# An attention and feed-forward kernel: the one-element tile of its first exponential moves into a longer identity tile, and every large buffer starts at another address

## The chip, the cores and the metric

The kernel runs on one core of a Trainium2 chip. The time is the device time of one execution in microseconds (us); a measurement is the median of several runs. TensorE, VectorE, ScalarE, GpSimd and SyncE are written PE, DVE, ACT, POOL and SP, as in the profile. The on-chip buffer (SBUF) has 128 partitions. A tile has the same address in all of them, and all addresses below are bytes from the start of a partition.

## The reference

Eight batches, eight heads, 576 tokens, head dimension 64, all in fp32. First 32 packed queries attend over the keys, then the tokens attend over the 32 packed results, and a feed-forward layer with a SiLU follows:

```
def sm_attn(qq, kk, vv):
    s = scale * np.matmul(qq, kk.transpose(0, 1, 3, 2))
    s = s - np.max(s, axis=-1, keepdims=True)
    a = np.exp(s)
    a = a / (np.sum(a, axis=-1, keepdims=True) + 1e-09)
    return np.matmul(a, vv)
p_packed = sm_attn(p, k, v)
out = sm_attn(q, p_packed, p_packed)
...
h = x @ w_in                      # x: 4608 x 512, w_in: 512 x 2048
g = h * (1.0 / (1.0 + np.exp(-h)))
return (g @ w_out)                # w_out: 2048 x 512
```

Here `x` is `out` with the heads side by side, so that the two large products of the feed-forward layer do most of the arithmetic. The weights `w_in` and `w_out` come in as 64-bit floats.

## The kernel before, in words

**Tiling.** A batch's 576 tokens are two halves of 288. The feed-forward dimension of 2048 is 16 slices of 128. The kernel multiplies the packed results of a batch with `w_in` once (`Packs.products`, L221) and gets the tiles `pw_hi` and `pw_lo`: fp32 values split in two parts, so that one product is made of three matmuls (high with high, high with low, low with high). A unit of work is one batch and one slice of 128:

- `h_products` (L501) makes the hidden values of the 2 x 288 tokens in PSUM. The stationary operand is a 128x128 block of `pw_hi` or `pw_lo`; the moving one is a row of 288 columns of `a2_hi` or `a2_lo`, the attention's shares. For a half these are six matmuls, three for `par` 0 and three for `par` 1, and `par` picks the first or the second 288 columns of the `a2` tile.
- `h_values` and `h_lower` (L519 to L526) apply the SiLU on ACT and split the result into `g_hi` and `g_lo`, on ACT and DVE.
- `out_products` (L533) adds the slice to the output sums in `ps_acc`. The stationary operand is a 128x128 block of `g_hi` or `g_lo`; the moving one is a row of 512 columns of `wo_hi` or `wo_lo`.

**Stages.** The first part, up to about 140 us, loads the weights in chunks (`Weights.fetch`, L183), turns the 64-bit floats into fp32 on ACT and DVE (L189 to L202) and splits `w_out` into `wo_hi` and `wo_lo` (L210, L214). Beside this run the attention of the first batches and the units of the first eight blocks. From then on the feed-forward units of a batch run with steps of the next batch's attention between them. The attention of every batch but the first spreads its turned exponentials with 16 small DMAs (`spread1`, L298) between two `tm` tiles, in runs of 256 bytes.

**Order.** PE, DVE, ACT and SP run in the order in which the program is written (`manual_schedule`): the string `ORDER` for the first part, a loop over units after it. POOL adds two halves of the weights now and then (L202). Nothing in that order depends on a tile's address.

**Where the tiles lie.** A pool's tiles are laid out in the order of the pools and of the tiles in them, one after the other, each rounded up to 32 bytes. The pool `const` comes first: `ident` (L109, 512 bytes), `win` (L111), `wo_hi` and `wo_lo` (L112, L113), `rest` (L115), and `ready` (L118, 4 bytes, in 32). Behind it lie `kvq`, `pw`, `a2p`, `tmp`, `small`, `gp`, `osb`, and the weights' staging buffer `w_raw`, in whose place `pw_b` and `gp_b` lie later. The one instruction that uses `ready` is the first exponential (L119), whose result nothing reads: it makes ACT load its table while the first data is on its way.

Of the kernel before, what the change touches and what calls it, by code (L numbers as in the profile page):

```python
# [9 lines left out]
F32 = mybir.dt.float32  # L10
# [9 lines left out]
P = 128  # L20
# [61 lines left out]
def packed_attention_ffn(ctx: ExitStack, tc: tile.TileContext, pkT, qT, v, w_in, w_out, out):  # L82
# [15 lines left out]
    const = ent(tc.tile_pool(name="const", bufs=1))  # L98
# [7 lines left out]
    ps_acc = ent(tc.tile_pool(name="ps_acc", bufs=2, space=PSUM))  # L106
    ps_two = ent(tc.tile_pool(name="ps_two", bufs=2, space=PSUM))

    ident = const.tile([P, P], F32, name="ident")  # L109
    make_identity(nc, ident)  # L110
    win = const.tile([P, NF, NI, P], I32, name="win")  # L111
    wo_hi = const.tile([P, NF, DM], F32R, name="wo_hi")  # L112
# [2 lines left out]
    rest = const.tile([P, NF, 2, 2, REST], F32, name="rest")  # L115
    parts = tc.dram_tile((EARLY, 2, P, 2, DM), F32, name="parts")

    ready = const.tile([P, 1], F32, name="ready")  # L118
    nc.scalar.activation(ready, ident[:, :1], AF.Exp)  # L119

    made = {}
# [638 lines left out]
```

## Time and profile before

| what | value |
|---|---|
| median of 3 runs | 719.77 us (719.29 to 721.39) |
| the profiled execution: its time | 719.32 us |
| the profiled execution: its span, first to last instruction | 717.5 us |
| PE busy | 700.1 us, 98% of the span |
| weight loads on PE busy | 569.1 us, 79% |
| DVE, ACT, POOL busy | 332.9, 331.5 and 17.0 us |
| moved by DMA | 65.20 MB |

The span lies 1.8 us under the execution's own time. Busy time of PE overlaps itself, because a matmul starts while the one ahead of it still drains; how fast PE goes is read from the distance between two starts. The order of the chain of waits shows what each moment of the time waited for.

### The profile page before, as it was taken

To read this page: it belongs to the slowest core of one execution; us is meant where nothing else is said; L and a number is where in the kernel's file an instruction comes from. 1 tells how busy PE (TensorE), PEld (TensorE's weight loads), DVE (VectorE), ACT (ScalarE), POOL (GpSimd) and SP (SyncE) were. 2 spreads that over 40 slices of the span, in tenths; PEclk is the share of its full clock that TensorE was granted. 3 is DMA by queue.
4 is the path that set the end of the run, shared out by engine and by line. 5 is a ranking of instruction groups with operands and counts; after the bars stand their busy time and mean duration, and the time that the engine had idled before them with its cause. 6 is when DMAs were issued, how large, how long until landed. Compare 5 with 4: busy or idle time off the path is not lost.

```text
span 717.5 us, 12182 instructions
## 1 busy us (share of the span) xinstructions
PE 700.1 (98%) x5094; PEld 569.1 (79%) x5094; DVE 332.9 (46%) x506; ACT 331.5 (46%) x619; POOL 17.0 (2%) x16
## 2 busy tenths in 40 slices
PE   7889999999999999999999999999999999999997
PEld 5667788888868888878878888878878788788885
DVE  5899867676342236332552315433362333622112
ACT  4788776555234325362532625453353533533221
POOL 0102011010000000000000000000000000000000
PEclk9799999999999999999999999999999999999999
DMA  9666542803032130312212122122301210010002
GB/s 356 273 234 247 190 185 80 297 22 118 1 132 81 34 144 1 124 23 82 74 60 81 20 84 74 40 86 40 139 1 62 78 35 1 1 59 1 0 1 73
DMA packets 30869, 65.20 MB, mean 91 GB/s; under 512 B 19296, under 2 KB 19296, under 8 KB 26464
## 3 DMA queue, kind: packets, MB, share of 16 engines
q1 hardware_dynamic: 30720, 64.30, 25.8%
q8 instruction: 40, 0.66, 0.4%
q10 hardware_dynamic: 96, 0.13, 0.1%
q14 instruction: 13, 0.11, 0.0%
HBM read 48.76 MB, written 11.53 MB: 84 GB/s over the span
## 4 chain that ended last, share of the span: by engine, by line
PE 92%; DVE 3%; DMA 2%; ACT 1%; SPq 1%; issue 1%; POOL 0%; ACTq 0%; DVEq 0%
PE ps_acc L533 56%; PE ps_two L501 27%; PE ps_two L221 6%; PE ps_two L319 2%; DMA w_raw<-in_w_in 1%; DMA win<-in_w_out 1%; SPq L298 1%; DVE w_raw L195 0%; DMA tm<-tm 0%; DVE tm L424 0%; DVE on_tokens L400 0%; PE ps_acc L371 0%; DVE on_tokens L421 0%; DVE win L195 0%; ACT L519 0%
## 5 line engine op out<-in xcount | busy, mean ns | idle before, releaser
L533 PE MATMUL ps_acc<-wo_hi,g_hi 128*128 128x512 f32 x576 | 231.9, 403 | 0.0
L533 PE MATMUL ps_acc<-wo_lo,g_hi 128*128 128x512 f32 x576 | 227.6, 395 | 0.0
L533 PE MATMUL ps_acc<-wo_hi,g_lo 128*128 128x512 f32 x576 | 227.6, 395 | 0.0
L526 DVE TENSOR_TENSOR g_lo<-g,g_hi 128x512 fp32r<-128x512 f32 (+1 forms) x132 | 88.7, 672 | 267.0 <-ACT g_hi L520 267.0
L519 ACT ACTIVATE g<-ps_two 128x512 f32<-128x512 f32 (+1 forms) x132 | 77.5, 587 | 270.1 <-PE ps_two L501 247.1
L501 PE MATMUL ps_two<-a_hi,pw_hi 128*128 128x288 f32 x512 | 151.8, 297 | 0.0
L501 PE MATMUL ps_two<-a_hi,pw_lo 128*128 128x288 f32 x512 | 151.8, 296 | 0.0
L501 PE MATMUL ps_two<-a_lo,pw_hi 128*128 128x288 f32 x512 | 151.4, 296 | 0.0
L533 PEld LDWEIGHTS ps_acc<-wo_hi,g_hi 128*128 128x128 f32 x576 | 108.0, 188 | 41.9 <-issue 20.8
L533 PEld LDWEIGHTS ps_acc<-wo_hi,g_lo 128*128 128x128 f32 x576 | 108.2, 188 | 26.2
L533 PEld LDWEIGHTS ps_acc<-wo_lo,g_hi 128*128 128x128 f32 x576 | 108.2, 188 | 20.5 <-DVE wo_lo L214 0.4
L501 PEld LDWEIGHTS ps_two<-a_hi,pw_hi 128*128 128x128 f32 x512 | 96.6, 189 | 6.2 <-ACT tm L247 0.9
L501 PEld LDWEIGHTS ps_two<-a_lo,pw_hi 128*128 128x128 f32 x512 | 96.6, 189 | 4.0
L501 PEld LDWEIGHTS ps_two<-a_hi,pw_lo 128*128 128x128 f32 x512 | 96.7, 189 | 0.0
L520 ACT ACTIVATE g_hi<-ps_two 128x512 fp32r<-128x512 f32 (+1 forms) x132 | 76.7, 581 | 9.9 <-PE ps_acc L533 9.9
L473 DVE TENSOR_TENSOR pw_lo<-ps_two,pw_hi 128x1024 fp32r<-128x1024 f32 (+1 forms) x35 | 38.5, 1127 | 13.9 <-ACT pw_hi L470 13.9
L470 ACT CAST pw_hi<-ps_two 128x1024 fp32r<-128x1024 f32 (+1 forms) x35 | 31.9, 943 | 25.5 <-PE ps_two L221 25.5
L221 PE MATMUL ps_two<-win,ppT 64*32 64x512 f32 (+1 forms) x560 | 33.3, 564 | 4.1 <-ACT rest L521 2.5
L521 ACT ACTIVATE rest<-ps_two 128x64 f32<-128x64 f32 (+1 forms) x132 | 30.2, 229 | 0.0
L221 PEld LDWEIGHTS ps_two<-win,ppT 64*32 64x32 f32 x560 | 8.2, 107 | 18.4 <-issue 10.7
L519 ACT ACT_TABLE_LOAD x17 | 21.8, 1283 | 2.2 <-PE ps_two L501 1.9
L189 ACT ACTIVATE w_raw<-w_raw 128x1024 int32<-128x1024 uint32 (+1 forms) x13 | 13.3, 1023 | 7.4 <-DMA w_raw<-in_w_in 5.5
(104 smaller groups left out, 446.0 us busy)
## 6 DMA issues: line engine op xcount, KB each, us to landing
kvq_t<-in_v SPq DMA_DIRECT2D x8, 1280.0 KB, 6.8
kvq_t<-in_pkT SPq DMA_DIRECT2D x7, 1216.0 KB, 5.9
out<-o SPq DMA_DIRECT2D x16, 512.0 KB, 2.8
kvq_t<-in_qT SPq DMA_DIRECT2D x7, 1152.0 KB, 5.2
w_raw<-in_w_in SPq DMA_DIRECT2D x6, 1024.0 KB, 7.7
win<-in_w_out SPq DMA_DIRECT2D x3, 1024.0 KB, 4.8
w_raw<-in_w_out SPq DMA_DIRECT2D x3, 1024.0 KB, 6.9
tm<-tm SPq DMA_DIRECT2D x56, 40.0 KB, 2.0
```

The costliest lines, as they stand in the source:

```text
L189: nc.scalar.activation(low, low.bitcast(U32), AF.Copy, scale=2.0**-29)
L221: nc.tensor.matmul(bank(par)[NP * i : NP * i + NP], lhs(r, i), rhs(r, i), start=True, stop=True)
L298: nc.sync.dma_start(self.e1T[NP * at : NP * at + NP, : some.shape[1], i], some)
L319: nc.tensor.matmul(self.ps[NP * i : NP * i + NP, par * D : par * D + D], e, vs[:n, c, h * D : h * D + D], start=(c == 0), stop=(c == 4),)
L470: nc.scalar.copy(self.hi, self.ps[:, :, : self.nf * P])
L473: nc.vector.tensor_tensor(self.lo, self.ps[:, :, : self.nf * P], self.hi.bitcast(F32), ALU.subtract)
L501: nc.tensor.matmul(bank, p[:, par, cols], a[:, par], start=(n == 0), stop=(n == len(todo) - 1))
L519: nc.scalar.activation(g, ps[..., :MAIN], AF.Silu)
L520: nc.scalar.activation(g_hi, ps[..., :MAIN], AF.Silu)
L521: nc.scalar.activation(to, ps[..., MAIN:HS], AF.Silu)
L526: nc.vector.tensor_tensor(g_lo[:, c], g[:, c], g_hi[:, c].bitcast(F32), ALU.subtract)
L533: nc.tensor.matmul(bank, g[:, rows], w[:, f], start=(first and n == 0), stop=(last and n == 2))
```

## The change

The tile `ident` gets 352 more fp32 columns (1408 bytes). The first of these is now `ready`, the target of the first exponential; the rest is not used. The tile `ready` is gone, and with it 32 bytes behind `rest`.

```diff
-    ident = const.tile([P, P], F32, name="ident")
+    ident = const.tile([P, P + 352], F32, name="ident")
+    ready = ident[:, P : P + 1]
+    ident = ident[:, :P]
     make_identity(nc, ident)
     win = const.tile([P, NF, NI, P], I32, name="win")
...
-    ready = const.tile([P, 1], F32, name="ready")
     nc.scalar.activation(ready, ident[:, :1], AF.Exp)
```

Both programs hold the same instructions in the same order with the same waits on all five engines. The single row that reads differently is the first exponential, which writes `ident` in place of `ready`; it has the same single wait, for POOL. Lines from L120 on are one higher in the changed file. What moves is where the tiles start:

| tile | start before | over a multiple of 256 | start after | over a multiple of 256 |
|---|---|---|---|---|
| `ident` | 16512 | 128 | 16512 | 128 |
| `win` | 17024 | 128 | 18432 | 0 |
| `wo_hi` | 49792 | 128 | 51200 | 0 |
| `wo_lo` | 82560 | 128 | 83968 | 0 |
| `rest` | 115328 | 128 | 116736 | 0 |
| `kvq_t` (first of 2) | 123552 | 160 | 124928 | 0 |
| `pw_hi` (first of 2) | 144032 | 160 | 145408 | 0 |
| `a2_hi` (first of 4) | 160416 | 160 | 161792 | 0 |
| `tm` (first of 2) | 178848 | 160 | 180224 | 0 |
| `g_hi` (first of 2) | 192160 | 160 | 193536 | 0 |
| `o` (first of 2) | 202400 | 160 | 203776 | 0 |
| `w_raw` (first of 2) | 210592 | 160 | 211968 | 0 |

The four tiles behind `ident` move by 1408 bytes, all tiles from `kvq_t` on by 1376. The buffers in a pool follow each other at their own sizes, which are multiples of 256 for all of these, so that the second and later ones lie like the first. Inside a tile not every row starts at such a multiple: the second 288 columns of an `a2` tile start 1152 bytes behind its beginning, which is 128 over a multiple of 256.

## Prediction

> **What bounds the kernel now.** I read the page's totals and its chain of waits first, then the chain in order of time, then the groups of instructions with different shapes kept apart. The totals, and the chain by engine and by line:
>
> ```profile
> span 717.5 us, 12182 instructions
> PE 700.1 (98%) x5094; PEld 569.1 (79%) x5094; DVE 332.9 (46%) x506; ACT 331.5 (46%) x619; POOL 17.0 (2%) x16
> PE 92%; DVE 3%; DMA 2%; ACT 1%; SPq 1%; issue 1%; POOL 0%; ACTq 0%; DVEq 0%
> PE ps_acc L533 56%; PE ps_two L501 27%; PE ps_two L221 6%; PE ps_two L319 2%; DMA w_raw<-in_w_in 1%; DMA win<-in_w_out 1%; SPq L298 1%; DVE w_raw L195 0%; DMA tm<-tm 0%; DVE tm L424 0%; DVE on_tokens L400 0%; PE ps_acc L371 0%; DVE on_tokens L421 0%; DVE win L195 0%; ACT L519 0%
> ```
>
> 92% of the chain is PE, and 83% is two lines: the output products L533 and the hidden products L501. DVE and ACT are busy for less than half the span. How fast the two lines go is read from the chain in order of time (start, length, what), how many they are from the groups:
>
> ```profile
> 303.00 3.19 PE ps_two L501 x24
> ...
> 693.67 19.61 PE ps_acc L533 x84
> ```
>
> ```profile
> L533 PE MATMUL ps_acc<-wo_hi,g_hi 128*128 128x512 f32 x576 | 231.9, 403 | 0.0
> ...
> L501 PE MATMUL ps_two<-a_hi,pw_hi 128*128 128x288 f32 x512 | 151.8, 297 | 0.0
> ```
>
> A matmul of L533 takes 19.61 / 84 = 0.2335 us and one of L501 3.19 / 24 = 0.133 us. Each line has three such groups of equal count, so there are 1728 and 1536 of them: 403 + 204 = 607 us of the 717.5. A nanosecond on each of these matmuls would be 3.3 us. The rest of the time has its slack at the beginning. The busy time of each engine in stretches of the span (PE, its weight loads, DVE, ACT, POOL, then the granted clock, the DMA share and GB/s):
>
> ```profile
> 0.00:30.00 30.00, 23.30 (x286) 17.65 (x286) 20.15 (x42) 17.44 (x33) 2.79 (x8) 0.91 0.88 351
> 30.00:60.00 30.00, 26.19 (x261) 19.61 (x261) 27.59 (x48) 23.95 (x48) 4.04 (x3) 0.91 0.69 243
> ...
> 300.00:500.00 200.00, 200.00 (x1459) 163.69 (x1460) 78.02 (x120) 84.89 (x166) 0.00 (x0) 1.00 0.21 65
> ```
>
> PE is idle for 6.7 + 3.8 = 10.5 us in the first 60 and not at all from 300 to 500. So an address can matter in two ways: through the pace of PE's reads, for 607 us, or through the DMAs and the chain of DVE and ACT in the first 60 us.
>
> **The change part by part.** Nothing is added or taken away: the order and the waits are the same on all engines. The first exponential costs what it did. Its row (shortest, median and longest ns, start), and two rows of the waits (who waited for whom: us in total, times, longest):
>
> ```profile
> L119 ACT ACTIVATE ready<-ident x1: 203/203/203, 2.0 to 2.0; 128x1 f32<-128x1 f32 x1
> ```
>
> ```profile
> ACT w_raw L189 <- DMA w_raw<-in_w_in: 5.5, 1, 5.5
> ...
> ACT g L519 <- PE ps_two L501: 247.1, 75, 7.3
> ```
>
> It is 203 ns at 2.0 us, and behind it ACT waits 5.5 us for the first weights, so it would cost nothing at five times the length. What is left is the addresses.
>
> *DVE and ACT.* The trace holds a comparison: before, `win` starts 128 over a multiple of 256 and so at a multiple of 64, while `w_raw` starts 160 over, 32 past a multiple of 64. The same instructions run on both (count, busy us, mean ns):
>
> ```profile
> L195 DVE SCALAR_TENSOR_TENSOR w_raw<-w_raw 128x1024 int32<-128x1024 int32 x9 | 11.0, 1227 | 0.3
> ...
> L190 ACT ACTIVATE w_raw<-w_raw 128x1024 f32<-128x1024 f32 x9 | 10.5, 1162 | 0.0
> ...
> L195 DVE SCALAR_TENSOR_TENSOR win<-win 128x1024 int32<-128x1024 int32 x3 | 3.7, 1226 | 0.1
> ...
> L190 ACT ACTIVATE win<-win 128x1024 f32<-128x1024 f32 x3 | 3.5, 1180 | 0.0
> ```
>
> DVE takes 1226 against 1227 ns, and ACT is 18 ns slower on the better aligned one. Multiples of 256 do not occur, but where 64 does nothing I take nothing for 256. These engines also have cover: ACT waits 247.1 us for L501. Term: 0.
>
> *PE's reads.* Here too the trace holds a comparison, inside L501. With `a2_hi` 160 over a multiple of 256, the 1152 bytes of `par` 0 touch six pieces of 256 bytes; those of `par` 1 begin 32 over and touch five. Six matmuls in a row are three of `par` 0 and three of `par` 1. In the timeline of PE these are the first of each three:
>
> ```profile
> 303.63 0.29 PE L501 MATMUL ps_two<-a_hi,pw_hi 128*128 128x288 f32 x1
> ...
> 304.03 0.29 PE L501 MATMUL ps_two<-a_hi,pw_hi 128*128 128x288 f32 x1
> ...
> 304.43 0.30 PE L501 MATMUL ps_two<-a_hi,pw_hi 128*128 128x288 f32 x1
> ...
> 304.83 0.29 PE L501 MATMUL ps_two<-a_hi,pw_hi 128*128 128x288 f32 x1
> ...
> 305.23 0.30 PE L501 MATMUL ps_two<-a_hi,pw_hi 128*128 128x288 f32 x1
> ...
> 305.63 0.29 PE L501 MATMUL ps_two<-a_hi,pw_hi 128*128 128x288 f32 x1
> ...
> 306.03 0.40 PE L533 MATMUL ps_acc<-wo_hi,g_hi 128*128 128x512 f32 x1
> ```
>
> Every step is 0.40 us, with six pieces (303.63, 304.43, 305.23) or five (304.03, 304.83, 305.63). Term: 0. It is bounded on the gain's side by the two paces: 224 more columns take 233.5 - 133 = 100.5 ns, 0.449 ns each, and 512 of them 229.7, so 3.8 ns of a matmul do not go with its columns. If all of that were the price of the start, moving or stationary, it would be 3.8 ns x 3264 = 12.4 us.
>
> *DMA.* All buffers that are filled or emptied by DMA move from 128 or 160 over to a multiple of 256. Windows of 5 us of the fill (the last two columns are the DMA engines' share and GB/s), the DMAs that stand in the chain, and an issue's size and median us to landing:
>
> ```profile
> 5.00:10.00 5.00, 3.71 (x51) 2.46 (x36) 2.77 (x6) 2.32 (x5) 0.00 (x0) 1.00 1.03 412
> ...
> 15.00:20.00 5.00, 3.49 (x56) 2.32 (x64) 3.94 (x8) 3.58 (x7) 0.00 (x0) 0.80 1.03 410
> ```
>
> ```profile
> 1.66 6.00 DMA w_raw<-in_w_in
> ...
> 41.42 5.53 DMA win<-in_w_out
> ...
> 52.12 1.93 DMA tm<-tm
> ```
>
> ```profile
> tm<-tm SPq DMA_DIRECT2D x56, 40.0 KB, 2.0
> ```
>
> The engines are full at 410 GB/s, so a shorter packet would show. If a row that starts off a multiple of 256 costs one more piece, a row of 4096 bytes (the first chunk of the weights) goes from 17 pieces to 16, one of 8192 (`win`) from 33 to 32, and one of 256 (`tm`) from two to one. In the chain that is at most 6.00 / 17 = 0.35, 5.53 / 33 = 0.17, and for the 40 KB of a `tm` DMA, 0.1 us at 410 GB/s, half of that: together 0.6 us. From below it is 0, if starts cost nothing. No buffer of before starts at a multiple of 256, so no row decides; I take the middle, -0.3. Beyond this sum, the upper bound of a gain is PE's whole wait for the spread of the second batch, which the smaller packets might end sooner; the waits say:
>
> ```profile
> PE ps_two L319 <- DMA tm<-tm: 1.2, 1, 1.2
> ```
>
> After it PE would wait for nothing but its own order, so this bound is 0.6 + 1.2 = 1.8 us. After 60 us DMA is under half busy and hidden under PE.
>
> [...]
>
> **Sum.** 0 + 0 + 0 - 0.3 us. The profiled execution of 719.32 us (span 717.5 and 1.8 around it) becomes 719.0, and the median of 719.77, 0.45 above that execution, becomes 719.5.
>
> **The rivals.** *Faster, because PE's reads pay for the start.* If one more piece of 256 bytes costs the 3.8 ns, L533 (nine pieces of `wo` before, eight after) saves 1728 x 3.8 = 6.6 us and `par` 0 of L501 768 x 3.8 = 2.9 us: 710.3. For it: the 3.8 ns exist. Against it: the equal steps of 0.40 us, where three pairs would differ by 11 ns each, a little over the last digit. The stationary blocks (512 bytes of `pw` or `g`, three pieces before and two after) have no such comparison in the trace. Chance 0.07.
>
> *Faster through the fill.* A gain of 2.2 us needs more than the DMAs in the chain and PE's wait for `tm` give together (1.8 us): DVE and ACT would have to get ahead too, in the 10.5 us in which PE idles. If half of these go, 714.5. Chance 0.04.
>
> *Slower: moving and stationary reads meet.* PE reads both operands at the same time. Before, `wo_hi` lies 640 over a multiple of 2048 and `g_hi` 1696, 1056 apart; after, 0 and 1024, so that both start at multiples of 256. If equal starts collide, each matmul of L533 gets longer. L501 already reads such pairs (`pw_hi` and `a2_hi` both lie 672 over a multiple of 2048), and its time per column is 133 / 288 = 0.462 ns against 233.5 / 512 = 0.456. At L501's rate L533 takes 236.5, 3.0 ns more, x 1728 = 5.2 us: 725.0. It decides from 2.2 us / 1728 = 1.25 ns each. Against it: the constant 3.8 ns explains the two rates without a collision, and all buffers behind `rest` keep their distances to each other, so that but for `ident` only `win`, `wo` and `rest` move against the others, by 32 bytes. Chance 0.06.
>
> *The change does nothing at all:* the DMA's packets are as long as before, 719.8. This is the sum's lower bound and within the same verdict.
>
> **How the numbers follow.** A measurement of this kernel tells a difference of about 0.3%, 2.2 us, from no change: 717.6 and 721.9 are the limits. My case, with everything between no gain and 1.8 us of gain, has 0.83, and all of it lies inside them. The rivals have 0.07 + 0.04 on the faster side and 0.06 on the slower. The range of the likeliest case: its bound 719.77 - 1.8 = 718.0, less the 0.5 us by which the fastest run of before lies under the median, 717.5; and on the other side no gain and the highest run of before, 721.4. It leaves out the 0.17 of the rivals, so it is the range of the forecast too.
>
> **What would show it right or wrong.** Right: L533 at 0.2335 us and L501 at 0.133 us in the chain, DVE L195 at 1226 ns, the same waits, and in the windows of the fill either the same GB/s (no gain) or some per cent more, with the chain's DMA pieces of 6.00, 5.53 and 1.93 us down by no more than 0.6 in sum. Wrong: a pace of L533 that differs by over 1.25 ns (84 matmuls in less than 19.50 or more than 19.71 us), three matmuls of L501 that no longer take 0.40, or an idle time of PE in the first 60 us that falls from 10.5 to under 8.

## The result, and the profile after

The changed kernel takes 712.15 us (median of 4 runs, 710.63 to 715.05) against 719.85 of the kernel before (4 runs, 719.29 to 721.39): a ratio of 0.989, 95% interval 0.986 to 0.993. It is 7.7 us faster where no change was forecast.

The profiled execution took 715.05 us, the slowest of the four, with a span of 713.2. The chain in order of time of the changed kernel (start, length, what; L501 is now L502, and L533 is L534):

```profile
1.66 6.07 DMA w_raw<-in_w_in
...
100.56 3.19 PE ps_two L502 x24
...
407.79 3.19 PE ps_two L502 x24
410.98 2.77 PE ps_acc L534 x12
413.75 1.60 PE ps_two L502 x12
415.35 2.73 PE ps_acc L534 x12
...
689.89 19.09 PE ps_acc L534 x84
```

The same places in the chain of the kernel before, beside the rows shown already:

```profile
98.83 3.20 PE ps_two L501 x24
...
408.46 3.19 PE ps_two L501 x24
411.65 2.79 PE ps_acc L533 x12
414.44 1.59 PE ps_two L501 x12
416.03 2.79 PE ps_acc L533 x12
```

The hidden products have not moved: 3.19 us for 24. The output products have: the last 84 take 19.09 us in place of 19.61, 227.3 ns each in place of 233.5, and a dozen 2.73 or 2.77 in place of 2.79. The row of L502 x24 that stood at 98.83 now stands at 100.56, 1.73 us late; the last matmul ends at 708.98 in place of 713.28, 4.30 early. So PE has won 6.0 us in between. The means of the steps between two starts in a dozen of L533, over all 143 dozens of 12 in the trace and without some 40 first steps of over 300 ns, are 233.0 ns before and 228.7 after: 4.3 ns x 1728 = 7.4 us, nearly the whole difference of the medians. A part of it is lost again in one wait: at 148.8 us PE waits 0.9 us for lower parts of `w_out`, where before only its weight load waited, 0.4 us. This wait is no part of the gain's cause; e2 below has the same pace without it, and in e3 it is 1.25 us:

```profile
PE ps_acc L534 <- DVE wo_lo L215: 0.9, 1, 0.9
```

The 1.73 us that this execution lost at the beginning go with its clock. The stretch from 30 to 60 us of the changed kernel (the clock is the third number from the end; before it was 0.91), and a row of its chain from the middle of that stretch, where six matmuls take 0.477 us each:

```profile
30.00:60.00 30.00, 27.31 (x254) 20.64 (x253) 26.08 (x45) 22.58 (x46) 2.08 (x2) 0.80 0.66 242
```

```profile
43.33 2.86 PE ps_acc L534 x6
```

From 40 to 50 us the granted clock was 0.66, where it was 1.00 before. The other three executions had mean clocks of 0.993 to 0.998 against 0.987, and 710.63 to 713.03 us.

What the forecast said of the other engines and of DMA can be read from the groups of the changed kernel and its windows of the fill:

```profile
L191 ACT ACTIVATE w_raw<-w_raw 128x1024 f32<-128x1024 f32 x9 | 10.4, 1158 | 0.0
...
L196 DVE SCALAR_TENSOR_TENSOR win<-win 128x1024 int32<-128x1024 int32 x3 | 3.7, 1226 | 0.1
```

```profile
5.00:10.00 5.00, 3.49 (x50) 2.38 (x35) 2.69 (x6) 2.25 (x5) 0.00 (x0) 1.00 1.03 414
15.00:20.00 5.00, 3.40 (x56) 2.15 (x64) 4.03 (x8) 3.68 (x7) 0.00 (x0) 0.83 1.02 415
```

DVE takes 1226 ns as before, ACT 1158 where it took 1162, the fill runs at 414 and 415 GB/s where it ran at 412 and 410, and the first DMA in the chain takes 6.07 us where it took 6.00. The pieces of 5.53 and 1.93 us do not stand in this chain, which follows other work there. PE is idle for 6.7 + 2.7 = 9.4 us in the first 60, where it was 10.5.

### The profile page after: what moved, and what is told of

Same layout as the page of the kernel before. It is cut to its first block, busy times and chain, and to the rows that moved or that the text cites. A ratio compares the mean times of both kernels' runs of the same rounds, so it can differ in the third digit from the quotient of the medians.

```text
span 713.2 us, 12182 instructions
## 1 busy us (share of the span) xinstructions
PE 696.0 (98%) x5094; PEld 571.3 (80%) x5094; DVE 333.6 (47%) x506; ACT 331.7 (47%) x619; POOL 17.0 (2%) x16
## 3 DMA queue, kind: packets, MB, share of 16 engines
q1 hardware_dynamic: 30720, 64.30, 24.8%
## 4 chain that ended last, share of the span: by engine, by line
PE 88%; DVE 5%; ACT 2%; DMA 2%; issue 1%; POOL 0%; SPq 0%; ACTq 0%; DVEq 0%
PE ps_acc L534 54%; PE ps_two L502 27%; PE ps_two L222 6%; DMA w_raw<-in_w_out 1%; PE ps_two L320 1%; DMA w_raw<-in_w_in 1%; DVE w_raw L196 1%; DVE w_raw L195 1%; DVE win L202 1%; ACT w_raw L191 0%; DVE win L196 0%; ACT L520 0%; DVE wo_lo L215 0%; DVE g_lo L527 0%; ACT w_raw L190 0%
## 5 line engine op out<-in xcount | busy, mean ns | idle before, releaser
L534 PE MATMUL ps_acc<-wo_hi,g_hi 128*128 128x512 f32 x576 | 229.6, 399 | 0.0
L534 PE MATMUL ps_acc<-wo_lo,g_hi 128*128 128x512 f32 x576 | 225.9, 392 | 0.9 <-DVE wo_lo L215 0.9
L534 PE MATMUL ps_acc<-wo_hi,g_lo 128*128 128x512 f32 x576 | 225.5, 392 | 0.0
L502 PE MATMUL ps_two<-a_hi,pw_hi 128*128 128x288 f32 x512 | 153.3, 299 | 0.1
L502 PE MATMUL ps_two<-a_lo,pw_hi 128*128 128x288 f32 x512 | 152.6, 298 | 0.0
L502 PE MATMUL ps_two<-a_hi,pw_lo 128*128 128x288 f32 x512 | 151.7, 296 | 0.0
L534 PEld LDWEIGHTS ps_acc<-wo_hi,g_hi 128*128 128x128 f32 x576 | 108.3, 188 | 40.7 <-issue 21.0
L534 PEld LDWEIGHTS ps_acc<-wo_hi,g_lo 128*128 128x128 f32 x576 | 108.4, 188 | 24.1 <-DVE g_lo L527 0.5
L534 PEld LDWEIGHTS ps_acc<-wo_lo,g_hi 128*128 128x128 f32 x576 | 108.4, 188 | 19.7 <-DVE wo_lo L215 1.2
L502 PEld LDWEIGHTS ps_two<-a_hi,pw_hi 128*128 128x128 f32 x512 | 97.5, 190 | 6.1 <-ACT tm L248 0.9
L502 PEld LDWEIGHTS ps_two<-a_lo,pw_hi 128*128 128x128 f32 x512 | 97.2, 190 | 3.4
L502 PEld LDWEIGHTS ps_two<-a_hi,pw_lo 128*128 128x128 f32 x512 | 97.3, 190 | 0.0
```

The costliest lines, as they stand in the source:

```text
L502: nc.tensor.matmul(bank, p[:, par, cols], a[:, par], start=(n == 0), stop=(n == len(todo) - 1))
L534: nc.tensor.matmul(bank, g[:, rows], w[:, f], start=(first and n == 0), stop=(last and n == 2))
```

## The experiments

The result left three theories. *Distance*: PE reads the moving row and a weight block, and what counts is how far apart the two tiles lie. `wo` and `g` were 1056 bytes apart over a multiple of 2048 and are now 1024; `a2` and `pw` moved together. *Moving start*: the row of `wo` must start at a multiple of 256. *Weight start*: the block of `g` must. Times are medians; the kernel before was run beside each group on the same chip and took 719.64 (first four), 719.90 (next four) and 719.87 us (the two after). "The 84" are the last 84 matmuls of L533 in the chain. The edits of e1 and e4 are against the kernel before, all others against the changed one; "..." marks lines left out.

### Four layouts that part the theories

`e1_wo_moves_alone`:

```diff
+    ident = const.tile([P, P + 352], F32, name="ident")[:, :P]
     ...
     ready = const.tile([P, 1], F32, name="ready")
```

> The identity tile stays 1408 bytes longer, but the tile `ready` is back behind `rest`: `win`, `wo` and `rest` start at multiples of 256 as in the changed kernel, all tiles behind them 32 bytes past one, and `wo` and `g` are 1056 bytes apart (over multiples of 2048) as before. Theory 1, the distance between the weight block of `g` and the moving row of `wo` counts: L533 stays at 0.2335 us, time 719 to 720. Theory 2, the moving row's own start counts: L533 at 0.2275, time 712. Theory 3, the weight block's start counts (a multiple of 64 or more): as before, 719 to 720.

720.10 us, ratio 1.0004 (0.9990 to 1.0017). The 84:

```profile
695.65 19.60 PE ps_acc L533 x84
```

The row of `wo` starts at a multiple of 256 and gains nothing. The moving start falls, and with it the rival of the prediction that had its gain from fewer pieces of 256 bytes.

`e2_distance_alone`:

```diff
-    ident = const.tile([P, P + 352], F32, name="ident")
+    ident = const.tile([P, P + 8], F32, name="ident")
```

> The identity tile is 32 bytes longer and holds `ready`: every large buffer starts 160 past a multiple of 256, as badly aligned as before or worse, but `wo` and `g` are 1024 apart as in the changed kernel. Theory 1 (distance): L533 at 0.2275 us in its long stretch at the end (84 matmuls in 19.1 us), time 711 to 713. Theories 2 and 3 (own start of the moving row or of the weight block): 0.2335 us (19.6 us), time 719 to 720.

712.60 us, ratio 0.9915 (0.9894 to 0.9936).

```profile
685.38 19.11 PE ps_acc L534 x84
```

Every large buffer starts 160 past a multiple of 256, as most did before, and the gain is there. 32 bytes in the identity's tile do what 1408 do.

`e3_all_at_64` is the changed kernel with `P + 368`:

> The changed kernel with 64 bytes more in the identity tile: every large buffer starts 64 past a multiple of 256, all distances as in the changed kernel. Theory 1 (distance): 0.2275 us per matmul, 711 to 713. Theory 2 (moving row at a multiple of 256): 0.2335 us, 719 to 720. Theory 3 (weight block at a multiple of 64): 711 to 713; at a multiple of 256: 719 to 720.

712.46 us, ratio 0.9904 (0.9889 to 0.9919), the 84 in

```profile
688.53 19.09 PE ps_acc L534 x84
```

`e4_distance_1088`:

```diff
+    ident = const.tile([P, P + 352], F32, name="ident")[:, :P]
     ...
-    ready = const.tile([P, 1], F32, name="ready")
+    ready = const.tile([P, 16], F32, name="ready")[:, :1]
```

> The long identity tile, and a `ready` of 64 bytes behind `rest`: `wo` starts at a multiple of 256, `g` 64 past one, 1088 apart, a multiple of 64 but not of 128. Theory 1: 711 to 713 if a distance of a multiple of 64 is enough, 719 to 720 if it takes 128 or more. Theory 2: 712. Theory 3: 712 if the weight block needs a multiple of 64, 719 to 720 if it needs 256.

719.67 us, ratio 1.0001 (0.9992 to 1.0011):

```profile
693.96 19.61 PE ps_acc L533 x84
```

In e3 and e4 `g` and all other tiles behind `rest` lie at the same addresses, 64 past a multiple of 256, and only `win`, `wo` and `rest` differ, by 64 bytes: one has the gain, the other hasn't. The weight start falls too. The distance is left, and a multiple of 64 is not enough.

### Which pair, and which distances

`e5_g_moves_alone`:

```diff
+    ent(tc.tile_pool(name="pad_g", bufs=1)).tile([P, 8], F32, name="pad_g")
     gp = ent(tc.tile_pool(name="gp", bufs=2))
```

> The changed kernel with 32 unused bytes between the `small` and the `gp` pool: `g`, `o`, `w_raw` and the late `pw` and `g` buffers start 32 past a multiple of 256, everything ahead stays. Theory 1a, the distance that counts is that of the two tiles that L533 reads (`wo` and `g`, now 1056): the gain is gone, 0.2335 us per matmul, 19.6 us for the last 84, time 719 to 720. Rival 1b, it is the distance of `wo`, `win` or `rest` to `kvq`, `pw`, `a2` or `tm`: the gain stays, 19.1 us, 712.

718.99 us, ratio 0.9985 (0.9975 to 0.9994):

```profile
694.37 19.61 PE ps_acc L535 x84
```

All tiles ahead of `g` lie as in the changed kernel, and the gain is gone but for 0.9 us, so the pair is `wo` and `g`, the two tiles that L533 reads. The first exponential writes `ident` here too, so that this part of the change has no share in the gain.

`e6_a2_off_by_32`:

```diff
+    ent(tc.tile_pool(name="pad_a", bufs=1)).tile([P, 8], F32, name="pad_a")
     a2p = ent(tc.tile_pool(name="a2p", bufs=4))
+    ent(tc.tile_pool(name="pad_b", bufs=1)).tile([P, 56], F32, name="pad_b")
```

> The changed kernel with 32 unused bytes ahead of the `a2` tiles and 224 behind them: `a2` is 32 off a multiple of 256 from `pw`, the tile that L501 reads with it, and `g` is 1280 in place of 1024 from `wo`. If every pair of reads has this price, L501 goes from 0.133 us per matmul to 0.1355 or more (the 2.6% of L533), which is 4 to 5 us; if its pace is set by something else, its rows stay at 3.19 us for 24. For L533: 1280 as good as 1024 if multiples of 256 are what counts (19.1 us for 84), 19.6 us if not. Time 712 to 713 with L501 unmoved and 1280 good; 716 to 717 with L501 slower; 719 to 720 with 1280 bad.

712.26 us, ratio 0.9886 (0.9866 to 0.9906). A run of the hidden products and the 84:

```profile
650.41 3.20 PE ps_two L504 x24
...
688.27 19.11 PE ps_acc L536 x84
```

For L533 a distance of 1280 is as good as 1024: 19.11 us against 19.09. L501, with `a2` 32 bytes further, stays where it was, 3.20 us against 3.19. That looked as if L501 had another limit; e9 and m1 show that it had not had its good pace before.

`e7_sweep_by_32` makes the `g_hi` and `g_lo` tiles `512 + 8` columns long, `e8_sweep_by_64` `512 + 16`, and reads the first 512.

> The changed kernel with every `g` buffer 32 bytes longer, so that the buffers lie at different distances from `wo`: `g_hi` 1024, 1056 and 1152, `g_lo` 1088, 1120 and 1184 in the three sets that take turns. Theory 1a: the units of one trace have different paces. The set with 1056 and 1120 has 0.2335 us or so; the set with 1024 and 1088 lies between (two loads of three are of `g_hi`); the third tells of 1152 and 1184. If multiples of 128 are enough, the third is as fast as the first. Rival, that a start or another pair counts: all units alike.

> The same with 64 bytes: `g_hi` at 1024, 1088 and 1280 from `wo`, `g_lo` at 1152, 1216 and 1344. Theory 1a with multiples of 256: the sets with 1024 and 1280 as `g_hi` are fast for the most part, the set with 1088 and 1216 has 0.2333. If multiples of 128 are enough, the set with 1024 and 1152 is at 0.2275 throughout. Rival: all units alike.

One run each: 718.21 and 717.29 us, the 84 in 19.50 and 19.46 us:

```profile
692.67 19.50 PE ps_acc L534 x84
```

```profile
691.77 19.46 PE ps_acc L534 x84
```

With the matmuls sorted by the set of buffers that their unit uses, the mean steps in e7 are 230.7 ns (1024 and 1088), 232.1 (1056 and 1120) and 233.4 (1152 and 1184): the units differ, as theory 1a had it, though the second set is not the slow one that it named. In e8 they are 231.6, 231.5 and 231.7, alike, where two sets should have been faster. That is what the rival said of e8; a start as the cause is excluded by e1 to e4, and another pair by e5. So a matmul's pace is not a matter of its own distance alone; a unit that mixes a good distance with another does not keep the good pace.

`e10_distance_1152` is e5 with 32 columns in the pad in place of 8:

> The changed kernel with 128 unused bytes ahead of the `gp` pool: `g` is 1152 from `wo`, a multiple of 128 and not of 256. If multiples of 128 are enough: 0.2275 us per matmul in the long stretch, 711 to 713. If it takes 256: 0.2335 us, 719 to 720; the sweep by 64, where such buffers were mixed with others and had 0.2315, speaks for something between.

718.61 us, ratio 0.9984 (0.9975 to 0.9994):

```profile
692.12 19.58 PE ps_acc L535 x84
```

A distance of 1152, a multiple of 128 and not of 256, is nearly as bad as 1056 and 1088: 19.58 us for the 84 against 19.61 in e5 and e4.

### A kernel that gives L501 the same distances

`e9_a2_rows_apart` is e2 with longer `a2` tiles:

```diff
-        hi = a2p.tile([P, 2, HS], F32R, name="a2_hi")
-        lo = a2p.tile([P, 2, HS], F32R, name="a2_lo")
+        hi = a2p.tile([P, 2, 320], F32R, name="a2_hi")[:, :, :HS]
+        lo = a2p.tile([P, 2, 320], F32R, name="a2_lo")[:, :, :HS]
```

> The kernel with the distance of `wo` and `g` mended by 32 bytes alone (1024 apart, no buffer at a multiple of 256), and with `a2` tiles whose second 288 columns begin 1280 bytes behind the first in place of 1152, so that every pair that L501 reads is a multiple of 256 apart, where it was 0 and 128 in turn. If L501's pace has the same price as L533's, its 0.133 us per matmul falls by 1 to 4 ns, which is 1.5 to 6 us: 706 to 711. If L501's pace is set by something else: 3.19 us for 24 as before and a time of 711 to 713.

712.45 us, ratio 0.9902 (0.9887 to 0.9917). Of its chain, and of that of e2 at the same place:

```profile
404.54 3.16 PE ps_two L502 x24
...
410.47 1.58 PE ps_two L502 x12
412.05 2.77 PE ps_acc L534 x12
```

```profile
403.19 3.19 PE ps_two L502 x24
...
409.15 1.60 PE ps_two L502 x12
410.74 2.73 PE ps_acc L534 x12
```

L501 does get faster: its mean step is 131.4 ns in place of 133.1 in e2, which is 2.6 us over the 1536 matmuls. But the dozen of L533 behind a single dozen of L501 now takes 2.77 where it took 2.73; there are 53 of these, which makes 2.1 us, and the time is that of e2 within the intervals. The gain is given back at the turn from the one to the other.

### The cost by itself

`m1_distances` leaves out attention and feed-forward layer. Its core is L533's order on two pairs of tiles, `at` bytes being added to the weight block's place:

```
for s, r in ((s_hi, w_hi), (s_hi, w_lo), (s_lo, w_hi)):
    nc.tensor.matmul(bank, s[:, block], r[:, f], start=True, stop=True)
```

> The disputed cost by itself. The attention and the feed-forward layer are left out; TensorE alone runs 84 matmuls of 512 columns in the order of L533 at each of eleven distances between the weight block and the moving row (0, 16, 32, 64, 96, 128, 160, 192, 224, 256, 512 over a multiple of 2048), then 72 of 288 columns at 0, 32, 64 and 128 and with 0 and 128 in turn. Theory 1a: 84 take 19.1 us at 0, 256 and 512 and 19.6 us at 32 and 64, with nothing else running; the others tell whether it is a step or a slope. Rivals, that the price comes from the other engines or from DMA: all eleven alike. For 288 columns: all alike (9.6 us) if another limit sets their pace.

The chain of this kernel in order of time; each row is one distance, named by its number of bytes:

```profile
22.33 19.05 PE zero L112 x84
...
61.35 19.88 PE thirtytwo L112 x84
...
81.27 19.87 PE sixtyfour L112 x84
...
121.19 19.80 PE onetwentyeight L112 x84
...
160.96 19.52 PE oneninetytwo L112 x84
...
200.44 19.36 PE twofiftysix L112 x84
...
219.85 19.39 PE fivetwelve L112 x84
...
239.29 9.76 PE short_zero L121 x72
...
249.09 9.88 PE short_thirtytwo L121 x72
...
268.94 9.87 PE short_onetwentyeight L121 x72
...
278.86 9.86 PE short_mixed L121 x72
```

The output is written beside the first two rows: the DMA engines are busy for 89% of `zero` and 43% of `sixteen`. From 61 us on nothing runs but PE, and the price is there (19.88 and 19.87 us at 32 and 64 bytes, 19.36 at 256): it is PE's own. Multiples of 256 are the good ones, `zero` with the DMA beside it like 256 and 512 without. The first step of a row of 512 columns is some 105 ns longer than the rest except at `zero`, which follows a warm-up at the same distance. Over the last 40 steps of each row the paces are 226.7 ns at 0, 256 and 512, 233.3 or 233.4 at 16, 32, 64, 160 and 224, 234.3 at 96, 232.4 at 128 and 229.0 at 192. At 256 and 512 the pace falls to 227 only after some ten steps between 224 and 240. With 288 columns it is 131.7 at 0 against 133.3 to 133.4 at 32, 64, 128 and with 0 and 128 in turn (`short_mixed`).

`m2_smaller_loads` makes the weight blocks smaller, and takes turns as the kernel does:

> Again TensorE alone, attention and feed-forward layer left out. First 84 matmuls of 512 columns with weight blocks of 128 columns at distances of 0, 4, 8 and 32 bytes, then with blocks of 64 and of 32 columns at 0 and 32. Theory 1a in the form that the reads of the weight block and of the moving row get in each other's way: the price of a bad distance (233.3 against 226.7 ns, 6.6 ns) goes with the size of the weight load, so about 3.3 ns with 64 columns and 1.7 with 32, and 4 and 8 bytes are as bad as 32. Rival, that the price belongs to the moving row or to the matmul as such: 6.6 ns with every block. Then eight turns of 12 matmuls of 288 columns and 12 of 512, as the feed-forward units have it, with the 512 at a distance of 0, 256, 512, 1024 and 32. In the changed kernel the first three of such a dozen take 232, 232 and 230 ns before they fall to 227: 256 to 1024 alike if multiples of 256 are all the same, and 32 higher throughout.

```profile
22.25 19.05 PE zero L113 x84
...
41.35 19.79 PE four L113 x84
...
61.19 19.70 PE eight L113 x84
...
80.93 19.87 PE thirtytwo L113 x84
...
100.85 19.55 PE half_zero L113 x84
...
120.44 19.69 PE half_thirtytwo L113 x84
...
140.18 19.66 PE quarter_zero L113 x84
...
159.88 20.32 PE quarter_thirtytwo L113 x84
...
186.48 2.73 PE turns_zero L113 x12
...
326.36 2.79 PE turns_thirtytwo L113 x12
```

All rows but `zero` hold a long first step, so the price is read from the last 40 steps again. It does not go with the size of the load: 231.6 - 229.8 = 1.8 ns with blocks of 64 columns, 240.0 - 231.7 = 8.3 with 32, 233.3 - 226.7 = 6.6 with 128. And smaller blocks at a distance of 0 are slower than full ones. 4 bytes have 232.4 ns and 8 bytes 230.7, worse than 0 and better than 32. The theory and the rival in the expectation both fall. The steps repeat in a short cycle (235 and 232 ns in turn at 32 bytes in m1); what makes them do so no run shows. The turns come out as in the kernel: 2.73 us a dozen at 0, 256, 512 and 1024 alike, 2.79 at 32.

## Why the prediction was wrong, point by point

- **What bounds the kernel: right.** 607 us are the two lines of PE, and a nanosecond on each matmul is 3.3 us. That is why 4.3 ns on one of them is 1% of the time.
- **Order and waits, the first exponential: right.** The exponential takes 203 ns at 2.0 us in both kernels, and e5 has it without the gain. The one new wait of PE, 0.9 us for `wo_lo`, costs time.
- **DVE and ACT, term 0: right**, 1226 ns and 1158 ns.
- **PE's reads, "Term: 0": the step that failed.** The comparison inside L501 held the pieces of 256 bytes against each other and showed truly that they cost next to nothing (over the whole trace three matmuls take 400.7 ns with six pieces each and 399.6 with five); e1 shows the same for L533. But it was read as if it held for an address altogether. What it left out is the distance between the two reads. In L501 that distance was 0 and 128 over a multiple of 256 in turn, and such a mixture has the slow pace throughout: 9.86 us for 72 in m1, against 9.76 at 0 alone. So the good distance was in the comparison and could not show. What the runs showed in place of 0 is 4.3 ns on each matmul of L533, 7.4 us. The bound of 12.4 us for PE's side did hold that, but by luck: it allowed 3.8 ns a matmul, and L533 won 4.3 on the mean and 6 in its long run, while L501 won nothing. And it was kept for a rival of 0.07 and out of the range.
- **DMA, -0.3: not to be seen in the time.** The fill's rate rose by about 1%. The DMA in the chain did not get shorter: the first piece takes 6.07 us, and where the other two stand in a chain again, e10 with `win` and `tm` at multiples of 256 has 5.44 and 1.91 us, and e9 with both 160 past has 5.39 and 1.93. And e2, with all buffers 160 past a multiple of 256, has the time of e3 and of the changed kernel within their intervals. The total of the DMA engines' time did fall. The queue's line of the kernel before and of the changed one:

```profile
q1 hardware_dynamic: 30720, 64.30, 25.8%
```

```profile
q1 hardware_dynamic: 30720, 64.30, 24.8%
```

  That is 25.8% of 717.5 = 185 us and 24.8% of 713.2 = 177 us per engine for the same bytes, hidden behind PE; e2 has 26.2% of 708.8 = 186, and e3, all at 64, 25.3% of 711.9 = 180. Most of it is in the packets of 256 bytes between the `tm` tiles: they take 21 ns at the median before and in e2, 18 in e3 and 15 in the changed kernel, while those of 4096 and 8192 bytes stay at 159 and 309. So a packet did get shorter, as this term had it, but not one that the time waits for. The -0.3 itself was the author's estimate: that a row starting off a multiple of 256 costs one more piece, from which it was worked out, no run shows, and none parts reads from writes. What the runs showed in its place is a packet of 256 bytes in 21, 18 and 15 ns with the tiles at 160, 64 and 0 past a multiple of 256, and 712.60 (e2), 712.46 (e3) and 712.15 us (the changed kernel) for the whole.
- **The rival "PE's reads pay for the start", 710.3 us:** near the time by luck, wrong in its mechanism. Its start of the moving row is made in e1, without a gain, and none of its starts in e2, with the whole gain.
- **The rival "Faster through the fill", 714.5 us:** did not come. PE's idle time in the first 60 us is 9.4 in place of 10.5, and the row at 100 us stands later than before, not earlier.
- **The rival "moving and stationary reads meet", 725.0 us:** the right pair of tiles, the right 32 bytes and the wrong sign. It took it that equal starts collide. The argument that L501 "already reads such pairs" was too loose: `par` 1 begins 1152 bytes further, so half of its pairs were 128 apart and its pace was the slow one all along (133.1 ns in e2, 131.4 in e9 without such pairs).

With PE alone at work (m1), it depends on where one read's tile lies against the other's whether a matmul takes 233.3 or 226.7 ns. What stays open is the mechanism below that. That the distance modulo 256 sets the pace, where all matmuls of a stretch share it, is shown by e2 against e1 (the 84 in 19.11 and 19.60 us), by e3 against e4 (19.09 and 19.61) and by m1 (226.7 ns at 0, 256 and 512, 229.0 to 234.3 at its other distances). That the two reads get in each other's way is only argued, and the simplest form of it, a price per column loaded, was refuted by m2. Why a mixed unit (e8) loses the pace, and why e9 loses at the turns what L501 gains, was not tried further. The 0.9 and 1.3 us that e5 and e10 keep (intervals that just exclude 1) are in part a slightly faster L533, 232.7 and 232.4 ns on the mean against 233.0, which is 0.5 and 1.0 us; why it is faster stays open.

## What to carry to other kernels

Where fp32r matmuls with a fresh weight block each bound a kernel, try to lay out the tile of the moving rows and the tile of the weight blocks a multiple of 256 bytes apart (here 1024 and 1280 took 19.09 and 19.11 us for 84 matmuls, 1056, 1088 and 1152 19.58 to 19.61), and look at the length of a long run of matmuls in the chain, not at their busy time. Begin with the pair of the longest runs: here that gave 1% of the time, and to add the pair of L501 in e9 gave nothing more (712.45 us against 712.60). Where the buffers begin on their own was worth nothing here: 32 bytes in the right place (e2, 712.60 us) gave what 1408 bytes of alignment gave (712.15). A comparison inside a trace excludes only what it varies: before a term is set to 0 by one, list which addresses, and which distances between them, it held fixed.

## What the runs showed of the hardware that was not expected

- A matmul of 512 fp32r columns with a weight load of 128 columns takes 226.7 ns at its best distance and up to 234.3 at others, with PE alone at work (m1); 288 columns take 131.7 and 133.3.
- The step is neither sharp nor even: 4 bytes off a multiple give 232.4 ns, 8 bytes 230.7, 32 bytes 233.3, 96 bytes 234.3, 192 bytes 229.0, a multiple 226.7 (m1 and m2, last 40 steps).
- The pace settles: behind a change of distance to 256 or 512 some ten matmuls of m1 pass, with steps between 224 and 240 ns, before 227 holds, and in the changed kernel the first three of a dozen take 232.6, 232.0 and 229.7 ns on the mean before it falls to 227 or 228.
- Smaller weight blocks are not faster: 229.8 ns with 64 columns and 231.7 with 32, against 226.7 with 128, all at a distance of 0 (m2), though their loads are shorter (134 and 109 ns on the mean against 188).
- A packet of 256 bytes between two SBUF tiles takes 15 ns at the median where the tiles lie at multiples of 256 (the changed kernel), 18 at 64 past one (e3) and 21 at 160 past one (the kernel before and e2).
